# ConvNeXt-V2 block on one core: for 14 of 128 row blocks the residual x is copied to the output first and the result is added to it by accumulating transfers

## The chip, the cores and the metric

The kernel runs on one core of a Trainium2 chip. The core has five engines that work side by side, each with an instruction queue of its own that is worked off in order: TensorE (PE, with its weight loads listed as PEld), VectorE (DVE), ScalarE (ACT), GpSimd (POOL) and SyncE (SP). Here SP only issues transfers. GpSimd computes and issues transfers too. All transfers, whoever issues them, are carried by the core's 16 DMA engines.

The metric is the device time of one execution in microseconds (us). The kernel before has a median of 1466.34 us over three runs (1464.90 to 1467.73).

## The reference

x is an image of 512 x 512 pixels with C = 96 channels in bf16, w1 is 96 x 384, w2 is 384 x 96, and E = 384.

```python
out = sum over i, j of xp[:, i:i+H, j:j+W, :] * dw[i, j]     # 3x3 depthwise convolution
h = _layernorm(out, axis=-1)
h = gelu(h @ w1)                                             # tanh form, 384 channels
gx = sqrt((h * h).sum(over all pixels) + 1e-6)               # one number per channel
nx = gx / (gx.mean(over channels) + 1e-6)
h = grn_gamma * (h * nx) + grn_beta + h
return x + h @ w2
```

The sum over all pixels splits the work: no output can be formed before the hidden values of the whole image have been seen once. The scaling by gamma * nx + 1 is folded into w2 (the tile W2s), and beta @ w2 is one row of 96 numbers (B2c). So an output pixel is x + B2c + gelu(...) @ W2s.

## The kernel before, in words

The image is cut into 128 blocks of four rows (GR = 4, 2048 pixels, 384 KB of x). On the chip an output block lies as 128 partitions x 16 pixels x 96 channels.

**First phase.** A loop runs over slots s = 0 to last_slot. In slot s the 3x3 convolution of block s is made by matmuls, and the later steps of earlier blocks: statistics, the norm on GpSimd (tile yn), four writes of yn to a DRAM buffer, one read back in another layout (ynT), then the first product with w1 and the gelu (mlp). Each step has a slot from a small planner in the code: a write comes one slot behind its norm, the read one slot later, the mlp two slots behind the read. In this phase every engine's queue keeps the order of the program. The last mlp (block 127) is planned for slot 141, so slots 128 to 141 have no convolution any more. In those 14 slots SP issues what is left of the rows and broadcasts of the norm, the yn writes, the ynT reads and the stores of kept hidden values (`store_next`, g_dram); in slot 139 also the first five loads of x for the second phase (`load_xr`), in slot 141 the first calls of `load_rest`.

**Between the phases** VectorE works out the scaled W2s.

**Second phase.** A loop runs over n = 0 to 127, with q = ORDER[n] the block. ORDER mixes blocks whose hidden values are made again from ynT (three spread reads of 128 KB each, then matmuls and gelu into gr), blocks whose hidden values were stored (`gl`, one load of 1536 KB issued by GpSimd), and five that stayed in SBUF. From about the thirtieth block on every third one is a stored one in most stretches. For each n the program issues:

- `load_rest` and `load_xr` for n + 5: the hidden values, and x into the tile xr (384 KB, issued by GpSimd, five buffers);
- `stage_xb` for n + 2: GpSimd adds B2c to xr and writes xb in f32 (three buffers);
- `stage_mm2` for n: per block 48 matmuls of 96 columns in four parts, and for each part one VectorE addition of PSUM and xb into o_sb (bf16, four buffers); between the parts `pace` has PE and ACT make hidden values for later blocks;
- `stage_out` for n - 1: the store of o_sb, issued by SP.

PE, DVE and ACT keep the program's order. From n = 8 on the queues of SP and GpSimd in this phase are ordered by the scheduler of the language, by its own estimates and the dependencies.

In the profile nearly all instructions carry line 35, because a helper records them; the lines of the second phase that differ are L283 (xr load), L294 (gl load), L328 (xb), L128 (ynT reads) and L356 (store).

Of the kernel before, what the change touches and what calls it, by code (L numbers as in the profile page):

```python
# [8 lines left out]
ALU = mybir.AluOpType  # L9
# [3 lines left out]
GR = 4  # L13
# [43 lines left out]
def kernel(  # L57
# [10 lines left out]
    nc = tc.nc  # L68
# [5 lines left out]
    B, H, W, C = x.shape  # L74
# [6 lines left out]
    NBLK = H // GR  # L81
# [31 lines left out]
    PXP = GR * W // 128  # L113
# [11 lines left out]
    def read_spread(eng, t, q):  # L125
        rows = yn_dram[q].rearrange("(c i) (r w) -> i c r w", i=NI, r=GR)
        for i in range(NI):
            eng.dma_start(out=t[i:128:4], in_=rows[i])  # L128

    def yn_dst(q, r):  # L130
        return yn_dram[q].rearrange("(c i) (r w) -> r c i w", i=NI, r=GR)[r]
# [17 lines left out]
    B2bc_f = consts.tile([128, C], f32, name="B2bc_f")  # L149
# [9 lines left out]
    grp = {}  # L159
# [6 lines left out]
    B2c = consts.tile([128, C], f32, name="B2c")  # L166
# [3 lines left out]
    ORDER = []  # L170
# [16 lines left out]
    with ExitStack() as p1:  # L187
        pe, dve, act, pool, sp = (InOrder(tc, e) for e in (nc.tensor, nc.vector, nc.scalar, nc.gpsimd, nc.sync))
# [18 lines left out]
        def out_bank():  # L207
            out_banks[0] += 1
            return PS[:, 7 - out_banks[0] % 2, :GPS * C].rearrange("p (g c) -> p g c", g=GPS)
# [36 lines left out]
        for b in range(min(2, NBLK)):  # L246
# [3 lines left out]
                       in_=zrow[:, None, :NI * GR * 32].to_broadcast([128, 3, NI * GR * 32]), func=ACTF.Identity)  # L250
# [25 lines left out]
        GPS = max(d for d in range(1, cap + 1) if PXP % d == 0)  # L276
        NSUB = PXP // GPS

        def load_xr(n, pq):
            q = ORDER[n]  # L280
            r0 = q * GR
            xr = late.xr.tile([128, PXP, C], bf16, name="xr")
            pq.dma_start(out=xr[:], in_=x[0, r0:r0 + GR].rearrange("r w c -> (r w) c").rearrange(  # L283
                "(p g) c -> p g c", g=PXP))
            grp.setdefault(q, {})["xr"] = xr
# [35 lines left out]
                    c += sz  # L321
            act.activation(out=g[:, t, :, :].rearrange("p j w -> p (j w)"), in_=Uf, func=ACTF.Gelu_apprx_tanh)

        def stage_xb(q, pq, bias):
            if q is None:
                return
            xb = late.xb.tile([128, PXP, C], f32, name="xb")
            pq.tensor_tensor(out=xb[:], in0=grp[q]["xr"][:],  # L328
                                    in1=bias[:, None, :].to_broadcast([128, PXP, C]), op=ALU.add)
            grp[q]["xb"] = xb  # L330

        def stage_mm2(n, q):
            g, xb = grp[q]["g"], grp[q]["xb"]
            GQ = QW // 128
            o_sb = late.o.tile([128, PXP, C], bf16, name="o_sb")
            for sub in range(NSUB):
                O = out_bank()
                for gl_ in range(GPS):
                    gg = sub * GPS + gl_
                    for j in range(NCH):  # L340
                        t, c = gg // GQ, gg % GQ * 128
                        pe.matmul(O[:, gl_, :], lhsT=g[:, t, j, c:c + 128], rhs=W2s[:, j, :],
                                   start=(j == 0), stop=(j == NCH - 1))
                dve.tensor_tensor(out=o_sb[:, sub * GPS:(sub + 1) * GPS, :], in0=O,
                                   in1=xb[:, sub * GPS:(sub + 1) * GPS, :], op=ALU.add)
                if n == NBLK - 1:
                    out_part(q, o_sb, sub)
                if sub == NSUB - 1 and q in nth_made:
                    used[0] += 1
                pace(n, sub)  # L350
            grp.pop(q)
            return o_sb

        def stage_out(q, o_sb):
            r0 = q * GR
            nc.sync.dma_start(  # L356
                out=out[0, r0:r0 + GR].rearrange("r w c -> (r w) c").rearrange("(p g) c -> p g c", g=PXP),
                in_=o_sb[:])

        PRE = 5  # L360
        LEAD = 6
# [12 lines left out]
        def pace(n, sub):  # L374
            soon = (n, sub + 2) if sub < NSUB - 1 else (n + 1, 1)
            due = sum(1 for v in todo if v < soon or v[0] < n)
            even = LEAD + (n * NSUB + sub + 1) * total / (NSUB * NBLK)
            advance(max(due, even), n + PRE)
# [22 lines left out]
        for i in range(NI):  # L401
            dve.tensor_tensor(out=Wd[:, i], in0=eye32[:, None, :].to_broadcast([128, 9, 32]),
                              in1=Ud[:, i, :, None].to_broadcast([128, 9, 32]), op=ALU.mult)
        n = 0
        for h in range(2):
            for j in range(GR):
                for q in (2 * h, 2 * h + 1):
                    a = q + GR * shift(h, j) - j + 1
                    if 0 <= a < 3:
                        n += 1  # L410
                        o, i_ = Wq[32 * q:32 * q + 32, :, :, j, :], Wd[32 * q:32 * q + 32, :, 3 * a:3 * a + 3, :]
# [141 lines left out]
        def stage_newton(k, eng):  # L553
            N = BATCHES[k][1] * GR * NG
            var, rcur = rns[k]
            for it in range(NEWTON_ITERS):
                last = it == NEWTON_ITERS - 1
                t_ = small.tile([128, NS], f32, name="nt")
                eng.tensor_tensor(out=t_[:, :N], in0=rcur, in1=rcur, op=ALU.mult)
                eng.tensor_tensor(out=t_[:, :N], in0=t_[:, :N], in1=var[:, :N], op=ALU.mult)  # L560
                eng.tensor_scalar(out=t_[:, :N], in0=t_[:, :N], scalar1=-0.5, scalar2=1.5, op0=ALU.mult, op1=ALU.add)
                rn = small.tile([128, NS], bf16 if last else f32, name="rstd" if last else "rn")
                if last and N % 32:
                    eng.memset(rn[:, N:(N + 31) // 32 * 32], 0.0)
                eng.tensor_tensor(out=rn[:, :N], in0=t_[:, :N], in1=rcur, op=ALU.mult)
                rcur = rn[:, :N]
            rns[k] = rn
# [80 lines left out]
        def stage_write(b):  # L648
            yn = yns.pop(b)
            for r in range(GR):  # L650
                sp.dma_start(out=yn_dst(b, r), in_=yn[32 * r:32 * r + 32, :, :])
# [17 lines left out]
        def flat(b):  # L669
            return gs[b].rearrange("p t j w -> p (t j w)")  # L670
# [82 lines left out]
        def store_next():  # L753
            if stores:
                b, h = stores.pop(0)
                n = NCH * QW * NQ // 3
                sp.dma_start(out=g_dram[whole.index(b)][:, h * n:h * n + n],
                             in_=flat(b)[:, h * n:h * n + n])
# [9 lines left out]
        def gram_next(n):  # L768
            for b, c0 in grams[:n]:
                for c1 in (c0, c0 + E):  # L770
                    for j in range(NCH):
                        v = flat(b)[:, c1 + j * 128:c1 + j * 128 + 128]
                        pe.matmul(gram[:, j, :], lhsT=v, rhs=v, start=False, stop=True, skip_group_check=True)
            del grams[:n]
# [63 lines left out]
        for s in range(last_slot + 1):  # L838
# [9 lines left out]
            for b in get("write"):  # L848
                stage_write(b)
            store_next()  # L850
            for k in get("newton"):
                stage_newton(k, pool)
            for b in get("sqp"):
# [105 lines left out]
            if s == last_slot - 2:  # L959
                for n in range(PRE):  # L960
                    load_xr(n, sp)
            if s == last_slot - 1:
                for n in range(3):
                    stage_xb(ORDER[n], pool, B2bc_f)
            if s == last_slot:
                for n in range(PRE):
                    load_rest(n, sp, sp)
        while stores:
            store_next()
        gsm = p2.enter_context(tc.tile_pool(name="gsm", side="right", bufs=1))  # L970
        gram_next(len(grams))
        aggregate(NACC - 1)
# [14 lines left out]
        r = gi[:].bitcast(f32)  # L987
        for it in range(3):
# [5 lines left out]
            r = rn_[:]  # L994
# [21 lines left out]
    with p2:  # L1016
        def out_part(q, o_sb, sub):
            r0 = q * GR
            nc.sync.dma_start(
                out=out[0, r0:r0 + GR].rearrange("r w c -> (r w) c").rearrange(  # L1020
                    "(p g) c -> p g c", g=PXP)[:, sub * GPS:(sub + 1) * GPS],
                in_=o_sb[:, sub * GPS:(sub + 1) * GPS])

        held = None
        FIRST = 8
        for n, q in enumerate(ORDER):
            sq, pq = (sp, pool) if n < FIRST else (nc.sync, nc.gpsimd)
            if n + PRE < NBLK:
                load_rest(n + PRE, sq, pq)
                load_xr(n + PRE, pq)  # L1030
            if 3 <= n + 2 < NBLK:
                stage_xb(ORDER[n + 2], pq, B2c)
            if n == NBLK - 1:
                stage_out(*held)
                held = None
            o_sb = stage_mm2(n, q)
            if held:
                stage_out(*held)
            held = (q, o_sb)


# [28 lines left out]
```

## Time and profile before

| | |
|---|---|
| median of three runs | 1466.34 us |
| the profiled execution's own time | 1466.53 us |
| its span, first to last instruction | 1464.7 us |
| time outside the span | 1.83 us |
| mean granted TensorE clock | 0.998 |
| PE / ACT / POOL / DVE busy in the span | 95% / 96% / 89% / 80% |
| second phase | from about 965 us to the end |

The page gives the busy time of each engine, its course over 40 slices, the transfer queues, the chain of work that ended last, the costliest groups of instructions and the DMA issues. q0 is the queue of the transfers that GpSimd issues, q1 that of SP. Busy shares over the whole span mix two phases with different limits, so the second phase and the last 14 slots of the first are read in windows of their own. A DMA share is the mean busy share of the 16 DMA engines in a window.

### The profile page before, as it was taken

The numbers are of one execution on the slowest core, as the hardware profiler recorded it, in microseconds if no ns is written. First come the engines' busy times: TensorE is split into PE (matmuls) and PEld (weight loads), VectorE is DVE, ScalarE is ACT, GpSimd is POOL, SyncE is SP. The second block draws the span as 40 slices with busy tenths as digits, with TensorE's granted clock in tenths as the row PEclk, the third lists the DMA queues.
The fourth block names the chain that finished last, engine by engine and source line by source line (L and its number), as shares of the span: only waits on it lengthen the run. The fifth ranks groups of instructions, "written<-read, shape, count | busy, mean of one in ns | idle before, by whom it ended". The sixth has DMA issues, their size and how long they took to land.

```text
span 1464.7 us, 54551 instructions
## 1 busy us (share of the span) xinstructions
PE 1392.0 (95%) x23155; PEld 812.2 (55%) x23155; DVE 1176.8 (80%) x2163; ACT 1404.4 (96%) x1595; POOL 1300.3 (89%) x923
## 2 busy tenths in 40 slices
PE   8889999999999999999999998799999999999998
PEld 3434444444444444444444445567777777777766
DVE  7859989999999999999999998755555555555555
ACT  6889999999999999999999999999999999999997
POOL 2569889999999999999899998469999999999997
PEclk9999999999999999999999999999999999999999
DMA  5577878888888888888878777569999999999997
GB/s 173 166 232 246 252 247 254 259 263 269 256 268 284 248 260 265 273 259 265 257 249 272 247 240 217 171 215 386 348 332 393 393 398 390 402 384 406 388 380 306
DMA packets 167770, 421.66 MB, mean 288 GB/s; under 512 B 34278, under 2 KB 84134, under 8 KB 163046
## 3 DMA queue, kind: packets, MB, share of 16 engines
q1 hardware_dynamic: 151284, 314.59, 65.3%
q0 software_dynamic: 14880, 103.43, 18.6%
q8 instruction: 182, 2.98, 0.8%
q14 instruction: 62, 0.51, 0.1%
q10 hardware_dynamic: 1362, 0.15, 0.1%
HBM read 261.77 MB, written 156.22 MB: 285 GB/s over the span
## 4 chain that ended last, share of the span: by engine, by line
DVE 37%; PE 27%; ACT 13%; POOL 12%; DMA 5%; issue 4%; SPq 1%; ACTq 0%; POOLq 0%; DVEq 0%
PE PS L35 27%; DVE bst L35 26%; POOL xb L328 10%; ACT g L35 8%; DVE xT L35 7%; ACT y_bf L35 2%; DMA out_dram<-o_sb 2%; ACT xT L35 1%; ACT gr L35 1%; SPq L35 1%; POOL xr L283 1%; DMA yn_dram<-yn 1%; DVE y_bf L35 1%; DMA xin<-in_x_dram 1%; DVE o_sb L35 1%
## 5 line engine op out<-in xcount | busy, mean ns | idle before, releaser
L35 ACT ACTIVATE g<-PS 128x512 bf16<-128x512 f32 (+2 forms) x1054 | 718.8, 839 | 13.3 <-PE PS L35 10.1
L35 DVE BATCH_NORM_STATS2 bst<-g 128x6 f32<-128x512 bf16 x1098 | 665.8, 671 | 24.8 <-ACT g L35 24.6
L35 ACT ACTIVATE gr<-PS 128x1536 bf16<-128x1536 f32 x364 | 503.3, 1461 | 15.6 <-PE PS L35 11.0
L35 DVE TENSOR_TENSOR o_sb<-PS,xb 128x384 bf16<-128x384 f32 x512 | 277.7, 556 | 223.2 <-PE PS L35 177.3
L35 POOL TENSOR_TENSOR yn<-y_bf,rbc 128x1536 bf16<-128x1536 bf16 x126 | 391.4, 3109 | 47.2 <-ACT rbc L35 22.8
L328 POOL TENSOR_TENSOR xb<-xr,B2c 128x1536 f32<-128x1536 bf16 x118 | 368.2, 3134 | 1.5
L35 PE MATMUL PS<-xT,Wq 64*32 64x511 bf16 (+1 forms) x9198 | 345.2, 387 | 22.9 <-ACT y_bf L35 6.9
L35 PE MATMUL PS<-ynT,w1p 128*128 128x512 bf16 x1167 | 332.8, 381 | 22.4 <-ACT g L35 4.8
L35 POOL TENSOR_TENSOR ysq<-y_bf 128x1536 bf16<-128x1536 bf16 x114 | 313.4, 2749 | 30.7 <-ACT y_bf L35 17.4
L35 PE MATMUL PS<-ynT,w1s 128*128 128x512 bf16 x1008 | 272.3, 379 | 0.0
L35 PEld LDWEIGHTS <-gr 128*128 128x128 bf16 x4332 | 214.3, 98 | 62.6 <-issue 5.5
L35 PE MATMUL PS<-W2s,gr 128*128 128x96 bf16 x4224 | 223.4, 206 | 4.4 <-DVE o_sb L35 4.3
L35 PEld LDWEIGHTS <-Wq 64*32 64x32 bf16 x9216 | 111.7, 90 | 192.8 <-issue 151.1
L35 ACT ACTIVATE y_bf<-PS 128x1536 bf16<-128x1536 f32 (+2 forms) x135 | 182.2, 1355 | 16.1 <-PE PS L35 14.0
L35 DVE STREAM_TRANSPOSE xT<-xin 128x576 f32<-128x576 f32 (+1 forms) x256 | 181.3, 747 | 13.9 <-DMA xin<-in_x_dram 13.9
L35 PEld LDWEIGHTS <-w1p 128*128 128x128 bf16 x1167 | 89.9, 97 | 177.1 <-issue 105.8
L35 PEld LDWEIGHTS <-g 128*128 128x128 bf16 (+1 forms) x1659 | 102.4, 98 | 87.1 <-issue 56.1
L35 PE MATMUL PS<-w1p,ynT 128*128 128x384 bf16 (+2 forms) x834 | 127.2, 273 | 9.2 <-ACT xT L35 4.2
L35 PE MATMUL PS<-g 128*128 128x128 bf16 x1416 | 119.4, 221 | 3.6 <-DVE PS L35 3.6
L35 PEld LDWEIGHTS <-w1s 128*128 128x128 bf16 x1008 | 81.0, 98 | 40.0
L35 PEld LDWEIGHTS <-gl 128*128 128x128 bf16 x1680 | 83.0, 98 | 28.5 <-issue 7.1
L35 PE MATMUL PS<-W2s,gl 128*128 128x96 bf16 x1680 | 90.2, 206 | 3.9 <-DVE o_sb L35 3.4
(109 smaller groups left out, 723.2 us busy)
## 6 DMA issues: line engine op xcount, KB each, us to landing
xin<-in_x_dram SPq DMA_DIRECT2D x126, 432.0 KB
g_dram<-g SPq DMA_DIRECT2D x105, 512.0 KB
gl<-g_dram POOLq DMA_DIRECT2D x35, 1536.0 KB, 10.9
yn_dram<-yn SPq DMA_DIRECT2D x512, 96.0 KB
ynT<-yn_dram SPq DMA_DIRECT2D x128, 384.0 KB
out_dram<-o_sb SPq DMA_DIRECT2D x127, 384.0 KB
xr<-in_x_dram POOLq DMA_DIRECT2D x123, 384.0 KB, 6.6
ynT<-yn_dram SPq DMA_DIRECT2D x252, 128.0 KB
```

Source lines behind the costliest of these rows:

```text
L35: r = f(*a, **k)
L283: pq.dma_start(out=xr[:], in_=x[0, r0:r0 + GR].rearrange("r w c -> (r w) c").rearrange("(p g) c -> p g c", g=PXP))
L328: pq.tensor_tensor(out=xb[:], in0=grp[q]["xr"][:], in1=bias[:, None, :].to_broadcast([128, PXP, C]), op=ALU.add)
```

## The change

For the 14 blocks with n = 12, 20, 28 and so on to 116 in the order of the second phase (12 <= n < 120 and n % 8 == 4):

- in each slot from 128 on, behind `store_next`, SP issues one copy of x to out, DRAM to DRAM, for one of these blocks (384 KB). There are 14 such slots and 14 blocks, so the loop that would issue leftover copies behind the slots finds none;
- `load_xr` and `stage_xb` do nothing for them: no load of x into SBUF, no GpSimd addition;
- the four VectorE additions take B2c, broadcast over the pixels, in place of xb;
- the store of o_sb is issued by GpSimd, not SP, and adds o_sb to what lies in out.

The other stores have the same bytes as before and are written with flattened rows of 1536 numbers.

```diff
+    def px_rows(ap, r0):
+        return ap[0, r0:r0 + GR].rearrange("r w c -> (r w) c").rearrange("(p g) c -> p (g c)", g=PXP)
...
+        def adds(n):
+            return 12 <= n < 120 and n % 8 == 4
+
+        copied = [q for n, q in enumerate(ORDER) if adds(n)]
+
+        def copy_x():
+            if copied:
+                r0 = copied.pop(0) * GR
+                sp.dma_start(out=px_rows(out, r0), in_=px_rows(x, r0))
+
         def load_xr(n, pq):
             q = ORDER[n]
+            if adds(n):
+                return
...
-        def stage_xb(q, pq, bias):
-            if q is None:
+        def stage_xb(n, pq, bias):
+            q = ORDER[n]
+            if adds(n):
                 return
...
                 dve.tensor_tensor(out=o_sb[:, sub * GPS:(sub + 1) * GPS, :], in0=O,
-                                   in1=xb[:, sub * GPS:(sub + 1) * GPS, :], op=ALU.add)
+                                   in1=B2c[:, None, :].to_broadcast([128, GPS, C]) if adds(n)
+                                   else grp[q]["xb"][:, sub * GPS:(sub + 1) * GPS, :], op=ALU.add)
...
-        def stage_out(q, o_sb):
-            r0 = q * GR
-            nc.sync.dma_start(
-                out=out[0, r0:r0 + GR].rearrange("r w c -> (r w) c").rearrange("(p g) c -> p g c", g=PXP),
-                in_=o_sb[:])
+        def stage_out(n, o_sb):
+            o, v = px_rows(out, ORDER[n] * GR), o_sb[:].rearrange("p g c -> p (g c)")
+            if adds(n):
+                nc.gpsimd.dma_start(out=o, in_=v, accum_op=ALU.add)
+            else:
+                nc.sync.dma_start(out=o, in_=v)
...
             store_next()
+            if s >= NBLK:
+                copy_x()
...
         while stores:
             store_next()
+        while copied:
+            copy_x()
```

More of the change, by code (lines that the diff above doesn't have):

```diff
@@ L332, in stage_mm2 @@
         def stage_mm2(n, q):
-            g, xb = grp[q]["g"], grp[q]["xb"]
+            g = grp[q]["g"]
             GQ = QW // 128
@@ L963 @@
                 for n in range(3):
-                    stage_xb(ORDER[n], pool, B2bc_f)
+                    stage_xb(n, pool, B2bc_f)
             if s == last_slot:
@@ L1031 @@
             if 3 <= n + 2 < NBLK:
-                stage_xb(ORDER[n + 2], pq, B2c)
+                stage_xb(n + 2, pq, B2c)
             if n == NBLK - 1:
@@ L1038 @@
                 stage_out(*held)
-            held = (q, o_sb)
+            held = (n, o_sb)
 _INS = ['x', 'dw', 'w1', 'w2', 'grn_gamma', 'grn_beta']
```

## The prediction

> **What bounds the kernel now.** I first read the busy times by stage, because the shares over the span mix two phases. Columns: window, its length, busy us (and instructions) of PE, PEld, DVE, ACT, POOL, then the granted clock, the DMA share and GB/s.
>
> ```profile
> 877.00:943.00 66.00, 53.17 (x484) 33.87 (x483) 55.16 (x101) 65.02 (x49) 38.18 (x25) 0.97 0.67 201
> ...
> 1000.00:1128.00 128.00, 128.00 (x1880) 95.29 (x1877) 72.77 (x134) 126.61 (x93) 122.03 (x71) 1.00 0.97 364
> 1128.00:1250.00 122.00, 120.01 (x1749) 88.79 (x1746) 67.13 (x125) 118.15 (x86) 118.25 (x72) 1.00 1.01 395
> 1250.00:1379.00 129.00, 126.68 (x1844) 93.64 (x1843) 70.96 (x132) 124.73 (x91) 125.06 (x77) 1.00 1.01 393
> 1379.00:1420.00 41.00, 37.64 (x547) 27.60 (x546) 20.95 (x39) 37.16 (x28) 39.07 (x24) 1.00 1.02 395
> 1420.00:1455.00 35.00, 35.00 (x518) 26.10 (x516) 19.69 (x37) 34.69 (x27) 34.32 (x20) 1.00 0.96 368
> ```
>
> The first row is the stage that gets the copies: ACT is busy 65.0 of 66 us, POOL 38, the DMA engines 0.67. The others are the second phase. Up to 1128 and behind 1420 PE is never idle. Between, it loses 1.99 us (122 - 120.01), 2.32 and 3.36: together 7.67. That is all that a relief of other engines can give, since no PE work changes. Who takes it is in the waits from 1020 to 1440 us (waiter, releaser, total us, times, longest), and in the chain that ended last, cut at two places (start, us, what):
>
> ```profile
> DVE o_sb L35 <- PE PS L35: 144.2, 261, 0.7
> DVE o_sb L35 <- POOL xb L328: 36.4, 46, 1.5
> ...
> PE PS L35 <- DVE o_sb L35: 7.3, 16, 2.0
> DVE o_sb L35 <- DMA out_dram<-o_sb: 6.6, 3, 3.1
> ```
>
> ```profile
> 1141.05 6.21 POOL xb L328 x2
> 1147.77 0.54 POOL xr L283
> 1148.32 3.13 POOL xb L328
> ...
> 1379.50 13.40 DMA out_dram<-o_sb
> 1392.96 10.03 DMA out_dram<-o_sb
> ```
>
> From 1129 to 1379 the chain runs mostly through POOL: additions back to back with DMA issues, DVE waits for xb, PE for DVE. That is 4.31 us of PE. From 1379 to 1415 it runs through three stores that land 10 to 13 us after issue and hold o_sb: 3.36 us. So two limits lie close together, and the DMA engines are full (1.01) during both.
>
> **The change part by part.** The sum is made against the profiled execution: 1466.53 us, of which 1464.7 are span and 1.83 lie outside it; it is 0.19 us above the median of 1466.34. PE's granted clock stays at 1.00 in these stages and is left alone.
>
> ```profile
> L328 POOL TENSOR_TENSOR xb<-xr,B2c 128x1536 f32<-128x1536 bf16 x64 | 199.6, 3134 | 0.7
> L283 POOL DMA_DIRECT2D xr<-in_x_dram x64 | 35.4, 554 | 7.1 <-POOL xb L328 7.1
> L294 POOL DMA_DIRECT2D gl<-g_dram x20 | 10.7, 533 | 0.0
> ```
>
> POOL, per changed block (the rows are of 1128 to 1379 us): it loses one addition of 3.13 us, one xr issue of 0.55 and some 0.1 to 0.3 of gap, and gains one accumulating issue. No row shows such an issue. The nearest are xr and gl at 0.55 and 0.53, the same for 384 and for 1536 KB; I take 0.55, and twice that, 1.1, as the upper end, nothing as the lower. Net 2.6 to 4.0 us, about 3.2 in eight blocks. PE's loss to POOL is 4.31 us in 251 us, some 64 blocks, so 0.54 in eight blocks. POOL stops being the limit at either end.
>
> The accumulating issue waits on POOL for the fourth DVE addition of its block. Behind it stand xb of the third block after it, which waits for the same addition already (three buffers), and the xr and gl issues. xr lands in 6.7 us and is used about three blocks (11.7 us) after issue; gl lands in 11.1 with two buffers at one use per three blocks. A wait of a few us is covered; without that cover DVE would wait for it as it now waits for xb.
>
> DMA engines: at 393 GB/s with the engines full, 393,216 bytes take 1.00 us. A changed block loses the xr load and the plain store, 2.00 us. The accumulating transfer reads o_sb, reads out and writes out. Its price is not in the trace: one pass (1.00, the second read hidden) to three (3.00, each paid alone). I take two, since a copy already reads and writes in one pass and there are two reads. Balance 0, ends -14 to +14 us of DMA time over 14 blocks. The Trainium skill has a price here: "Collectives: The Full Stack", in the section on the bandwidth ceiling and the fold count, says that an add in the DMA path costs no cycles of its own but two source reads, and gives 62.28 against 32.35 GB/s, 1.93 to one; by it, as an estimate, the balance would be -1 us. No run here shows it yet.
>
> What full DMA engines allow: from 1128 to 1379 they carried about 394 GB/s at POOL's pace. The best 50 us of the phase had
>
> ```profile
> 1250.00:1300.00 50.00, 48.88 (x713) 36.06 (x712) 27.59 (x51) 48.03 (x36) 48.37 (x30) 1.00 1.01 399
> ```
>
> At 399 the 251 us shrink by 251 x (1 - 394/399) = 3.1 us, of at most 4.31. Lower end 0, if 394 is already the limit. I take 3.1.
>
> The stores: 14 of 128 leave SP's queue, which waits 55.9 us for earlier stores from 1050 to 1440 us. The bytes stay, so of the 3.36 us lost behind 1379 I take back a quarter, 0.8 (ends 0 and 3.36).
>
> o_sb: it has four buffers, so the accumulating transfer must land before DVE's first addition four blocks later: three blocks of 3.9 us and a quarter, 12.7 us after o_sb is full. It is issued 0 to 6.2 us late (two xb in a row), then lands as xr does (4.5, 6.7, 8.8: least, median, most) or behind a gl (up to 12.0), plus up to 2 us for the further passes. I take 1 + 8.7, which fits: cost 0. The far end is 20 us, 7 too late. A late store cost PE 3.36 us for 6.6 us of DVE waiting, 0.51 per us, so that end is 14 x 7 x 0.51 = 50 us.
>
> DVE: 56 additions read a broadcast B2c in place of xb, both f32. I take the row of xb, 556 ns, as the same; even at twice that DVE, 55% busy here, has room. The plain stores' flattened form moves the same bytes: 0.
>
> The copies: SP issues one in each of 14 slots, 0.3 to 0.6 us by the rows of its other issues, behind this slot's write and ahead of the next slot's rows, broadcasts and reads. On the DMA engines one is 1.0 us (read and write in one pass) to 2.0, 14 to 28 us, against 66 x 0.33 = 22 idle. What they push back is a ynT read: issued at 932.40 for block 126, whose gelu starts about 942.8, so 10 us of cover, less landing, for which I take xr's least 4.5; the first of these reads, issued at 878.64, has some 9 us to its gelu. POOL already waits 3.7 us at most for a broadcast there and is half idle. I take 0; ends 0 and +6 (28 - 22). No gain is possible there: ACT is the limit.
>
> Sum: -3.1 - 0.8 = -3.9 us, span 1460.8, time 1462.6.
>
> **The rivals.**
> - Full relief: the accumulating transfer costs one pass, the DMA engines get 14 us back and PE runs without a gap: -7.67, so 1458.9. For it: PE is at 100% at 1000 to 1128 us, with 364 GB/s. Against it: two reads.
> - No change: 394 GB/s is the limit, PE's waits move from xb to o_sb: 1466.5, plus or minus 2.5. For it: DMA share 1.01 for 290 us, and SP's queue waiting longer for stores as the phase goes on. The Trainium skill speaks for it: "DMA: Bandwidth & Descriptors", on issuing engines not being separate queues, says that giving a transfer to another engine saves only issue time, as all share 16 engines. By that rule moving the stores to GpSimd gives nothing; the trace agrees so far as q0 with 56.4% and q1 with 43.0% fill the engines together (1050 to 1440 us).
> - Slower, by the buffer: the accumulating transfers land late and hold o_sb. At 2 us beyond the 12.7, 14 x 2 x 0.51 = 14.3, less 3.9: 1476.9. It decides from about 1 us beyond on (7 us, the gain and the 2.9 of the bound). For it: the store's landing is at that edge already (13.4). Against it: GpSimd's xr lands in 6.7.
> - Slower, by the engines: three passes, +14 on full engines and no relief: 1480.
> - Slower, in the first phase: the copies cost two passes and the tail pays 6: 1468.6, up to 1472.5 if the gain is absent too.
>
> **How the numbers follow.** About 0.2%, 2.9 us, is what a measurement of this kernel can tell from no change. The forecast has 0.34 (own range 1460 to 1463.4), full relief 0.11, no change 0.20, the late buffer 0.20, three passes 0.10, the first phase 0.05. Faster 0.45, same 0.20, slower 0.35. The range goes from 1458 (full relief) to 1479: it leaves out the worse half of the late buffer and most of three passes, under 2 in 10.
>
> **What would show it.** POOL between 1100 and 1400 us below 92% busy, and DVE's 36 us of waiting for xb nearly gone; the DMA share still about 1.0 and near 399 GB/s; PE over 99%; the accumulating issues at 0.55 us, landing under 12 us; slots 128 to 141 as long as before and the second phase starting at 965. I am wrong if DVE waits for DMA on o_sb by tens of us, if the landing is beyond 13 us, if GB/s falls while the share stays at 1, or if the second phase starts later.

## The result, and the profile after

| | before | after |
|---|---|---|
| median of six runs | 1466.52 us (1464.90 to 1467.73) | 1510.07 us (1505.04 to 1518.57) |
| profiled execution / its span | 1466.53 / 1464.7 us | 1513.52 / 1511.6 us |
| mean granted TensorE clock | 0.998 | 0.98 |

The ratio is 1.030, with a 95% interval of 1.0267 to 1.0333: the kernel became 43.6 us slower. The forecast was 1462.6 us, in a range of 1458 to 1479.

The windows by stage of the kernel after, with the columns of the table in the prediction:

```profile
877.00:943.00 66.00, 51.14 (x486) 32.47 (x485) 55.74 (x100) 65.24 (x51) 41.18 (x25) 1.00 0.81 236
...
1000.00:1128.00 128.00, 115.72 (x1645) 85.58 (x1642) 63.74 (x118) 111.05 (x81) 101.51 (x62) 0.95 0.88 308
1128.00:1250.00 122.00, 105.69 (x1451) 77.62 (x1450) 56.14 (x104) 98.38 (x72) 89.58 (x58) 0.93 0.89 318
1250.00:1379.00 129.00, 127.03 (x1870) 94.56 (x1868) 71.85 (x133) 126.02 (x92) 115.56 (x73) 1.00 1.01 383
1379.00:1420.00 41.00, 39.01 (x546) 28.65 (x543) 20.86 (x40) 36.94 (x28) 34.03 (x21) 0.96 1.00 360
1420.00:1455.00 35.00, 33.36 (x491) 24.68 (x489) 19.00 (x35) 33.17 (x25) 30.37 (x20) 1.00 1.02 389
```

Before, PE lost nothing up to 1128 us and 7.67 us from 1128 to 1420. Now it is idle for 12.28 us in the second row shown, 16.31 in the third, 1.97 and 1.99 in the next two: 32.6 us together. And where the granted clock is below 1.00 its busy time buys less: 105.69 us for 1451 instructions are 72.8 ns each, where it was 68.6 (120.01 / 1749). Over the rows at 0.95, 0.93 and 0.96 this is 1645 x 2.3 ns + 1451 x 4.2 + 546 x 2.6 = 11 us. So some 44 us are lost here by this estimate, where 7.67 were lost before.

Who takes it is in the waits of the kernel after from 1000 to 1490 us (waiter, releaser, total us, times, longest):

```profile
POOL xb L344 <- DVE o_sb L35: 51.4, 31, 8.5
...
DVE o_sb L35 <- DMA out_dram<-o_sb: 44.1, 12, 8.8
PE PS L35 <- DVE o_sb L35: 34.1, 9, 7.7
```

The wait of 36.4 us for xb, which the change was to relieve, is no longer among the large ones. In its place DVE waits 44.1 us for transfers that still hold o_sb (6.6 before), PE waits 34.1 us for DVE (7.3 before), and GpSimd itself stands idle behind DVE. Which transfers these are is in the tile's own instructions, L374 being the new issue:

```profile
L374 POOL DMA_DIRECT2D out_dram<-o_sb x14: 907/923/946, 1024.1 to 1468.8; - x14
...
  DVE o_sb L35: 42.1, 8
DMA to landing us min/median/max: 7.8/10.7/13.8
```

The first line gives the least, median and greatest time in ns that GpSimd spends on one issue. The second, under "who waited for it", gives 42.1 of the 44.1 us to these 14 transfers, and to eight of them. A landing of 10.7 us at the median is longer than the 8.7 of the forecast, and the longest, 13.8, is inside the 14 that it allowed (12.0 behind a gl, and 2 for further passes). So the landing alone doesn't explain waits of 8 us. The course of DVE around the first such wait shows what does (start, us, what, and in brackets the idle time before it with its releaser):

```profile
1019.00 0.56 DVE L35 TENSOR_TENSOR o_sb<-PS,B2c 128x384 bf16<-128x384 f32 x1 [0.29 <-DMA out_dram<-o_sb]
...
1022.17 0.56 DVE L35 TENSOR_TENSOR o_sb<-PS,B2c 128x384 bf16<-128x384 f32 x1 [0.63 <-PE PS L35]
...
1038.02 1.02 DVE L35 TENSOR_TENSOR o_sb<-PS,xb 128x384 bf16<-128x384 f32 x2 [7.90 <-DMA out_dram<-o_sb]
...
1071.87 1.02 DVE L35 TENSOR_TENSOR o_sb<-PS,xb 128x384 bf16<-128x384 f32 x2 [6.55 <-DMA out_dram<-o_sb]
```

The first two lines are block n = 12: its o_sb is full at 1022.73. The accumulating transfer is issued at 1024.14 and lands 13.76 us later, at 1037.90; DVE goes on at 1038.02. Counting the additions in fours, the addition at 1038.02 is the first of block 15, not 16. The one at 1071.87 belongs to block 22 and waits for the buffer of block 20. The buffer was used again three and two blocks later, while three other buffers should have come first. For all 14 blocks, read from the semaphore that the first addition of each later block waits for:

| block n | landing, us | next use of its buffer | DVE waits, us |
|---|---|---|---|
| 12 | 13.76 | n + 3 | 7.90 |
| 20 | 9.36 | n + 2 | 6.55 |
| 28 | 7.80 | n + 3 | none |
| 36 | 11.46 | n + 2 | 8.81 |
| 44 | 13.45 | n + 3 | 7.46 |
| 52 | 9.98 | n + 3 | 3.38 |
| 60 to 116 (8 blocks) | 9.2 to 13.1 | n + 4 | 2.10, 2.75, 3.14; else about none |

Where DVE had nothing else to wait for, the addition that needs the buffer came 3.3 us after o_sb was full for n + 2, 7.3 to 7.4 for n + 3 and 11.3 for n + 4. The six transfers that GpSimd issues 0.5 us behind a gl load (n = 12, 44, 60, 76, 92 and 108) land in 11.8 to 13.8 us, the other eight in 7.8 to 11.5.

The chain of work of the kernel after runs through just these (start, us, what):

```profile
1024.14 13.76 DMA out_dram<-o_sb
...
1062.39 9.36 DMA out_dram<-o_sb
...
1131.42 11.46 DMA out_dram<-o_sb
...
1172.63 13.45 DMA out_dram<-o_sb
```

What such a wait does to PE, in short windows of the kernel after around the first one:

```profile
1024.00:1030.00 6.00, 6.00 (x87) 4.38 (x85) 3.57 (x7) 5.87 (x5) 4.64 (x4) 1.00 1.02 347
1031.00:1038.00 7.00, 0.84 (x8) 0.32 (x6) 0.00 (x0) 2.29 (x2) 2.89 (x2) 0.80 1.01 337
1038.00:1042.00 4.00, 3.37 (x30) 2.53 (x30) 1.58 (x3) 0.93 (x1) 0.00 (x0) 0.50 0.46 187
1042.00:1046.00 4.00, 4.00 (x59) 2.94 (x58) 2.23 (x4) 3.25 (x4) 3.12 (x1) 1.00 0.28 102
```

PE is idle for 6.16 of 7 us, and then does 30 instructions in 3.37 us where it later does 59 in 4.00: the granted clock is 0.50 for the first 4 us behind the wait. The Trainium skill, "TensorE: Matmul & The Clock Gate", Part 1 on the HAM clock gate, says that an idle stretch of about 3.4 us halves the clock until about 3.4 us of activity have gone by. The trace agrees: 0.50 behind 7.9 us of waiting, 1.00 again 4 us later. So a wait of 8 us costs about 2 us more than itself, and one of 2 us, as before had them, doesn't.

The end of the first phase moved too. Before, then after: SP's loads of x, GpSimd's first three additions, and two groups of DVE's additions that lead to W2s.

```profile
938.20 2.26 SPq L35 DMA_DIRECT2D xr<-in_x_dram  x5
...
942.47 9.28 POOL L35 TENSOR_TENSOR xb<-xr,B2bc_f 128x1536 f32<-128x1536 bf16 x3 [16.44 <-DMA xr<-in_x_dram]
...
951.86 0.27 DVE L35 TENSOR_TENSOR parts<-mom 128x78 f32<-128x78 f32 x1
...
952.16 0.57 DVE L35 TENSOR_TENSOR parts<-parts,mom 128x78 f32<-128x78 f32 x2
```

```profile
947.02 2.35 SPq L35 DMA_DIRECT2D xr<-in_x_dram  x5
...
953.96 9.33 POOL L35 TENSOR_TENSOR xb<-xr,B2bc_f 128x1536 f32<-128x1536 bf16 x3 [21.15 <-ACT gr L35]
...
954.63 2.57 DVE L35 TENSOR_TENSOR parts<-mom 128x78 f32<-128x78 f32 x1
...
957.24 6.18 DVE L35 TENSOR_TENSOR parts<-parts,mom 128x78 f32<-128x78 f32 x2
```

SP issues the loads 8.8 us later, with twelve copies ahead of them in its queue. GpSimd's additions end at 951.75 before and at 963.29 after, and now lie beside DVE's, which take 8.75 us in place of 0.84. The first o_sb of the second phase is written at 962.33 before and at 971.61 after. The run-up of the profiled execution was already 3.5 us longer before any of the copies (up to slot 128 the profiles here differ from the one before by -0.5 to +4.9 us). What is left to the copies is some 6 us.

### The profile page after: what moved, and what is told of

Same layout as the page of the kernel before. It is cut to its first block, busy times and chain, and to the rows that moved or that the text cites. A ratio compares the mean times of both kernels' runs of the same rounds, so it can differ in the third digit from the quotient of the medians.

```text
span 1511.6 us, 54539 instructions
## 1 busy us (share of the span) xinstructions
PE 1404.9 (93%) x23155; PEld 820.2 (54%) x23155; DVE 1185.2 (78%) x2163; ACT 1404.8 (93%) x1595; POOL 1263.2 (84%) x909
## 4 chain that ended last, share of the span: by engine, by line
DVE 32%; PE 31%; ACT 14%; POOL 9%; DMA 8%; issue 4%; SPq 1%; ACTq 0%; DVEq 0%; POOLq 0%
PE PS L35 31%; DVE bst L35 22%; ACT g L35 9%; DMA out_dram<-o_sb 7%; POOL xb L344 7%; DVE xT L35 6%; ACT y_bf L35 3%; POOL xr L298 1%; DVE o_sb L35 1%; DMA yn_dram<-yn 1%; DVE y_bf L35 1%; ACT gr L35 1%; ACT xT L35 1%; DVE parts L35 1%; POOL yn L35 1%
## 5 line engine op out<-in xcount | busy, mean ns | idle before, releaser
L35 DVE TENSOR_TENSOR o_sb<-PS,xb 128x384 bf16<-128x384 f32 x456 | 247.7, 557 | 234.5 <-PE PS L35 190.1
L344 POOL TENSOR_TENSOR xb<-xr,B2c 128x1536 f32<-128x1536 bf16 x104 | 325.4, 3132 | 54.9 <-DVE o_sb L35 52.8
L35 PE MATMUL PS<-xT,Wq 64*32 64x511 bf16 (+1 forms) x9198 | 348.8, 391 | 24.0 <-ACT y_bf L35 7.8
L35 PE MATMUL PS<-ynT,w1s 128*128 128x512 bf16 x1008 | 278.1, 386 | 0.0
L35 PEld LDWEIGHTS <-gr 128*128 128x128 bf16 x4332 | 217.6, 99 | 68.4 <-issue 13.3
L35 DVE STREAM_TRANSPOSE xT<-xin 128x576 f32<-128x576 f32 (+1 forms) x256 | 181.5, 749 | 11.5 <-DMA xin<-in_x_dram 11.5
```

The lines of the kernel that those rows point to most:

```text
L35: r = f(*a, **k)
L344: pq.tensor_tensor(out=xb[:], in0=grp[q]["xr"][:], in1=bias[:, None, :].to_broadcast([128, PXP, C]), op=ALU.add)
```

## The experiments

There were three questions. Is it the time for which a buffer is held, and of that the early second use or the longer landing? What did the relief of GpSimd bring by itself? And do the copies cost DMA time, or their place in SP's queue? Times move by some us with the run-up, so beside each time stands the row of the profile that it should show in. A profile shows one execution; the times are medians of 4 to 12.

### A buffer of its own for the 14 blocks

The kernel after, with one more buffer that only the adding blocks use (eight blocks apart). To make room, a scratch tile is laid over another.

```diff
+                late.oa = p2.enter_context(tc.tile_pool(name="oa", side="right", bufs=1))
...
-            o_sb = late.o.tile([128, PXP, C], bf16, name="o_sb")
+            o_sb = late.oa.tile([128, PXP, C], bf16, name="o_add") if adds(n) else late.o.tile(
+                [128, PXP, C], bf16, name="o_sb")
...
-            junk = bstpool.tile([128, 128], f32, name="junk")
+            junk = zrow[:].bitcast(f32)[:, :128]
```

> The change with one more tile for the result: the 14 adding blocks write into a buffer of their own (o_add), which is used again only eight blocks later (31 us); the other blocks keep their four. The scratch of the three diagonal products is moved onto a tile that is no longer used, to make room. Theory H (the accumulating transfer holds a buffer of o_sb that the second or third block behind it is given, and lands 9 to 14 us after issue): DVE's 44 us of waiting for out_dram<-o_sb fall below 8, the granted clock in the second phase is back at 0.99 or more, time 1462 to 1469. Theory T (the accumulating transfers overload the DMA engines wherever their result lies): the waits move to loads or to the plain stores, time stays above 1490. Theory C (the copies at the end of the first phase cost the time): above 1490 too.

Measured: 1465.79 us against 1466.32 for the kernel before in the same series, ratio 1.0004 (0.9979 to 1.0029). The 44 us are gone with this edit alone. Its wait and its windows:

```profile
DVE o_sb L35 <- DMA out_dram<-o_sb: 1.3, 2, 0.7
```

```profile
1128.00:1250.00 122.00, 122.00 (x1791) 90.79 (x1788) 69.53 (x128) 120.82 (x88) 111.15 (x71) 1.00 1.02 392
1250.00:1379.00 129.00, 128.97 (x1895) 96.07 (x1894) 73.08 (x135) 127.44 (x94) 117.53 (x74) 1.00 1.02 394
1379.00:1420.00 41.00, 41.00 (x611) 30.72 (x608) 23.28 (x43) 40.65 (x31) 37.21 (x25) 1.00 1.02 400
```

PE is idle for 0.03 us in all three and its clock is 1.00 throughout, though the accumulating transfers still land in 7.5 to 12.8 us. So the transfers, the issues on GpSimd and the missing additions together cost nothing in this execution, and the whole 7.67 us that PE lost before from 1128 to 1420 come back. Something else must take them again, since the median is no better than before. The copies are the first suspect. They can't be all of it: the profiled execution took 1462.00 us, and others of this kernel up to 1476.09 at a lower granted clock (0.989 where this one has 0.995). What those lose is in no profile.

### The same room for the kernel before

The kernel before with the scratch tile laid over in the same way, and five buffers in the pool (`bufs=4` becomes `bufs=5`).

> The kernel before with five buffers of o_sb in place of four and nothing else of the change (the same scratch moved). H: a fifth buffer only takes away the late stores behind 1379 us, 0 to 3.4 us, so 1463 to 1466.5; the difference of the own-buffer kernel to the change is then not worth of a buffer as such. If the number of buffers were worth tens of us in general, this kernel would be far under 1460.

Measured: 1466.77 against 1466.32, ratio 0.9998 (0.9986 to 1.0010). A fifth buffer doesn't help the kernel before (the forecast's upper end was 1466.5), and so the gain of the last experiment is not owed to the room alone.

### A plain store by GpSimd

The kernel after, with the 14 stores still issued by GpSimd but without adding, so that these blocks lack x.

```diff
-                nc.gpsimd.dma_start(out=o, in_=v, accum_op=ALU.add)
+                nc.gpsimd.dma_start(out=o, in_=v)
```

> The change with a plain store by GpSimd in place of the accumulating one (x is left out of the output of the 14 blocks, since the store overwrites the copy); copies, queue and buffers stay. H in the form that the early reuse of the buffer is what hurts: a plain store lands as xr does, 6.7 us or up to 12 behind a gl, the reuse after two blocks comes 8 us behind, so DVE still waits some 5 to 25 us for out_dram<-o_sb, time 1470 to 1495. H in the form that the second read makes it late: waits under 5 us, time 1463 to 1469. T: as the latter.

Measured: 1492.48 against 1466.32, ratio 1.0183 (1.0162 to 1.0204), with this wait:

```profile
DVE o_sb L35 <- DMA out_dram<-o_sb: 27.4, 9, 5.5
```

and the landing of the 14 stores:

```profile
DMA to landing us min/median/max: 6.3/9.9/12.0
```

DVE still waits 27.4 us for transfers that hold o_sb, 23.4 of them for these 14 and up to 5.5 at a time; that is a little over the 25 that were expected at most. Against the kernel with the buffer of its own this is 26.7 us of the 44.3: more than half of the loss doesn't need the addition in the transfer; the longer landing of the accumulating transfer adds 17.6 us (1510.07 - 1492.48). And the buffers are given out as before: the first additions of blocks 15, 22, 31, 38, 47 and 55 wait for the same six stores as in the kernel after. So the early second use does not come from the adding.

### Buffers strictly in turn

The kernel after with its four buffers as four pools, block n using number n mod 4. Only the order of use is changed; all engines work off their instructions and transfers in the same order as in the kernel after.

```diff
-                late.o = p2.enter_context(tc.tile_pool(name="o", side="right", bufs=4))
+                late.o = [p2.enter_context(tc.tile_pool(name=f"o{i}", side="right", bufs=1)) for i in range(4)]
...
-            o_sb = late.o.tile([128, PXP, C], bf16, name="o_sb")
+            o_sb = late.o[n % 4].tile([128, PXP, C], bf16, name="o_sb")
```

> The change with its four o_sb buffers used strictly in turn (block n takes buffer n % 4), so that the buffer of an accumulating block is due again four blocks later in every case, where the change gave it to the second or third block behind for n = 12 to 52. Copies, accumulating transfers and their landing stay. Theory H2 (the early hand-out makes most of the loss): the DVE waits on out_dram<-o_sb fall from 44 us to 5 to 20, time 1470 to 1480. Rival L (the late landing alone is enough): waits of 30 us or more, time 1490 or more.

Measured: 1474.74 against 1466.86, ratio 1.0058 (1.0037 to 1.0079).

```profile
DVE o_sb L35 <- DMA out_dram<-o_sb: 18.1, 9, 3.4
```

With the second use four blocks later every time, 35.3 us of the loss are gone (1510.07 - 1474.74). What stays is six waits of 2.2 to 3.5 us (16.5 of the 18.1), for the transfers of blocks 12, 44, 60, 76, 92 and 108. These land 13.4 to 14.7 us after o_sb is full, and the addition four blocks later needs the buffer 11.3 us after it, not 12.7 as the prediction had it; the other eight land within 11.2. The waits cost about the 9.0 us between this kernel and the one with the buffer of its own (1474.74 - 1465.79). So of the loss of 44.3 us the early second use makes 35 and the landing 9, if the early use is taken away first. Taken in the other order, by the plain store, the longer landing makes 17.6 and the early use 26.7: the two add to each other's waits.

### The relief alone

The kernel after without the copies, and with the 14 blocks stored by SP. They have neither load of x nor GpSimd's addition, and so they lack x.

```diff
             if adds(n):
-                nc.gpsimd.dma_start(out=o, in_=v, accum_op=ALU.add)
+                nc.sync.dma_start(out=o, in_=v)
...
-            if s >= NBLK:
-                copy_x()
...
-        while copied:
-            copy_x()
```

> The relief alone: the 14 blocks load no x, have no xb and no copy, and are stored by SP with a plain store (x is left out of the output of these blocks). If POOL's additions and nothing else bound the stretch from 1129 to 1379 us, PE runs there without a gap and the time is 1458 to 1460; if the DMA engines share the bound, the 5.5 MB less of loads help as well and nothing can be told from the time alone, but PE's idle time shows the limit of the gain: 7.7 us.

Measured: 1458.77 against 1466.86, ratio 0.9949 (0.9932 to 0.9967): 8.1 us, within the measurement the 7.67 that PE lost to other engines before.

```profile
1128.00:1250.00 122.00, 122.00 (x1794) 90.86 (x1791) 69.29 (x128) 120.86 (x88) 107.52 (x67) 1.00 1.01 394
1250.00:1379.00 129.00, 128.07 (x1873) 95.03 (x1872) 72.07 (x134) 126.85 (x93) 113.39 (x70) 1.00 1.00 387
1379.00:1420.00 41.00, 40.38 (x596) 29.93 (x594) 22.70 (x42) 39.84 (x30) 33.40 (x22) 1.00 1.01 389
```

PE is full in the first row, with the DMA share still 1.01 at 394 GB/s, and loses 0.93 and 0.62 us in the others. So a share of 1.01 did not mean that the DMA engines bounded the stage. All 128 blocks are stored by SP here, and none of them shows an early second use: the first additions of blocks 15, 22, 31, 38 and 47 wait for no store of two or three blocks before. With the plain stores above this ties the early use to GpSimd as the issuer.

### The copies alone

The kernel before with 14 copies of x of the same size, in the same slots of SP's queue, into a DRAM buffer that nobody reads (px_rows stands here for its body, written out).

```diff
             store_next()
+            if s >= NBLK:
+                sp.dma_start(out=side[s - NBLK], in_=px_rows(x, 8 * (s - NBLK)))
```

> The kernel before with 14 copies of x by SP in slots 128 to 141, into a side tensor in DRAM that nothing reads; nothing else of the change. H: the second phase starts some 2.4 us later, as in the change (967.4 against 964.9 us), time 1467 to 1470. C: 1485 or more.

Measured: 1473.06 against 1466.32, ratio 1.0049 (1.0028 to 1.0070). Its end of the first phase:

```profile
946.03 3.08 SPq L35 DMA_DIRECT2D xr<-in_x_dram  x5
...
951.76 9.34 POOL L35 TENSOR_TENSOR xb<-xr,B2bc_f 128x1536 f32<-128x1536 bf16 x3 [19.21 <-DMA xr<-in_x_dram]
...
955.04 6.19 DVE L35 TENSOR_TENSOR parts<-parts,mom 128x78 f32<-128x78 f32 x2
```

The time is above the range of 1467 to 1470 and far under the 1485 of theory C. The copies by themselves, with the 2.3 us that the run-up adds, move SP's loads by 7.8 us and GpSimd's additions by 9.3, and DVE's pair of additions takes 6.19 us as in the kernel after. Set against matching ACT instructions of the kernel before, the stretch from slot 128 to the first o_sb is 4.5 us longer here, 3.9 in the kernel with its own buffer, 5.8 in the kernel after, 4.1 with the plain store and 3.0 with the buffers in turn.

### The copies later

The same bytes, two of the copies in the last two slots and twelve behind them, so that all stand behind the loads of x in SP's queue; once in the kernel with its own buffer, once as side copies in the kernel before.

```diff
-            if s >= NBLK:
+            if s >= last_slot - 1:
                 copy_x()
```

> The own-buffer kernel with the copies issued later: none in slots 128 to 139, two in slots 140 and 141, twelve behind the slots, so that SP issues the five xr loads of slot 139 ahead of all of them. Theory Q (a copy's cost is its place in SP's queue: xr lands 8 us later, GpSimd's three xb then run beside VectorE's additions on parts, which take 2.6 to 3.1 us in place of 0.27): the additions are back under 0.4 us, the second phase starts within 1 us of before, time 1458 to 1461. Rival B (the cost is the 14 us of DMA time or of HBM traffic, wherever the copies stand): the second phase still starts 4 us or more late, time 1464 to 1469.

Measured: 1462.08 against 1466.86, ratio 0.9964 (0.9947 to 0.9980). This kernel beats both, the one before by 4.8 us. The time lies between the ranges of the two theories, so it decides for neither; the rows do.

```profile
942.97 2.26 SPq L35 DMA_DIRECT2D xr<-in_x_dram  x5
945.27 14.38 SPq L35 DMA_DIRECT2D out_dram<-in_x_dram  x14
...
947.26 9.28 POOL L35 TENSOR_TENSOR xb<-xr,B2bc_f 128x1536 f32<-128x1536 bf16 x3 [17.13 <-DMA xr<-in_x_dram]
...
955.58 1.09 DVE L35 TENSOR_TENSOR parts<-mom 128x78 f32<-128x78 f32 x1
956.70 0.58 DVE L35 TENSOR_TENSOR parts<-parts,mom 128x78 f32<-128x78 f32 x2
```

All 14 copies are now issued in one stretch at the boundary, and yet two additions are short again; the first takes 1.09 us, since GpSimd's three end at 956.54. From the first of the last twelve gelus to the first o_sb it takes 25.05 us; the kernel before takes 25.07. (In the second phase of this execution PE loses 2.75 us between 1128 and 1250, where DVE waits for stores.)

> The kernel before with the 14 copies into a side tensor that nothing reads, at the late places (slots 140 and 141 and behind the slots); nothing else of the change. Q: 1465 to 1468, against 1473.06 with the copies in slots 128 to 141. B: 1470 to 1475.

Measured: 1470.94 against 1466.86, ratio 1.0024 (1.0012 to 1.0035).

```profile
956.22 0.27 DVE L35 TENSOR_TENSOR parts<-mom 128x78 f32<-128x78 f32 x1
956.52 0.57 DVE L35 TENSOR_TENSOR parts<-parts,mom 128x78 f32<-128x78 f32 x2
```

The additions are as short as before and the same stretch takes 25.07 us, so the boundary bears out the place in the queue. The time does not: it should have been 1465 to 1468, and it lies in the range of the rival B (1470 to 1475). The profiled execution was 4.4 us late from its first 107 us on, and in the second phase, which took 2.2 us longer, DVE waits longer for GpSimd than the 36.4 us of the kernel before:

```profile
DVE o_sb L35 <- POOL xb L329: 60.5, 62, 2.2
...
POOL xr L284 <- POOL xb L329: 17.2, 58, 0.3
```

The scheduler put GpSimd's instructions of the second phase in another order there: in four places a load of x and an addition changed places. That this order cost the rest is argued from the waits, not tested. The copies alone kept the order of the kernel before and DVE waited 47.3 us for GpSimd there. So how much of the 4.1 us is still the copies' stays open.

## Why the prediction was wrong

**The step that failed** is that of o_sb: "it has four buffers, so the accumulating transfer must land before DVE's first addition four blocks later ... 12.7 us", at a cost of 0. The pool gave the buffer of the first six adding blocks to block n + 2 or n + 3, which left 3.3 or 7.3 us. With the buffers strictly in turn the second use comes four blocks later, as the step assumed, and the time is 35.3 us lower; even then the addition needs the buffer after 11.3 us and not 12.7, so the bound itself was 1.4 us too wide. What gives the buffer out so early is not the adding: plain stores by GpSimd lose the same six buffers, and with all stores on SP none is lost. Why the language does so for stores issued by GpSimd, and why the distance becomes four from block 60 on, stays open.

**The landing** was taken as 1 + 8.7 us from o_sb full. Measured: issued 0.3 to 1.6 us after, landing with a median of 10.7 and up to 13.8, the long ones behind a gl load. The forecast's 8.7 was a load's 6.7 and 2 for the adding; a plain store by GpSimd takes 9.9 at the median, so the load was the wrong row to start from, more than the adding. Even with the buffers in turn, six of 14 exceed the bound. The rival "slower, by the buffer" gave 1476.9 for 2 us beyond; buffers in turn measured 1474.74, with waits of 2.2 to 3.5 us. So this rival was right in the place and in the price of such waits: they cost 9.0 us for 18.1 us of waiting, 0.50 per us against the 0.51 taken. That its sum comes near is partly luck, since it took 14 late transfers where there were six, a gain of 3.9 where 8.1 was there, and nothing for the copies. It should have had more of the chances: the store that already took 13.4 us in the chain of the kernel before was the row to go by, not GpSimd's loads of x.

**The price per us of waiting**, 0.51, came from waits of at most 3.1 us, part of which PE had work to cover. Here 44.1 us of waiting cost about 44: PE waited 34.1 of them, so about 1 us of each of the 12 waits was covered, and the halved clock added 11. With the plain store, 27.4 us of waits of up to 5.5 us cost about 27 against the buffer of its own. A price from short waits doesn't carry to long ones.

**The relief of GpSimd** was right in kind and too small: 3.1 and 0.8 us for POOL and the stores, where 8.1 came with the relief alone and PE was full in the profile of the kernel with the buffer of its own. The step that was mis-sized is "what full DMA engines allow", which held that 399 GB/s was a limit. The kernel with its own buffer reaches full PE at 392 to 400 GB/s, and POOL is 91% busy from 1128 to 1379 (228.7 of 251 us), under the 92% named. The rival "no change" falls with it. The rule that goes with that rival, that the issuing engine saves only issue time, isn't touched, since the gain came from additions and loads left out, and not from who issues the store.

**Accumulating as two passes** was right. By the trace's single packets of 3072 bytes, an accumulating one takes 252 ns at the median and a plain store's 121: 2.08 to one. The Trainium skill's figure in "Collectives: The Full Stack", section on the bandwidth ceiling, was 1.93; the trace puts it a little higher. The issue on GpSimd took 0.92 us, between the 0.55 taken and the end of 1.1; POOL had room for it. The additions with B2c took 556 to 559 ns, as taken.

**The copies** were put at 0 because DMA time and the ynT reads had cover. At the boundary of the phases they cost 3 to 6 us, inside the ends of 0 to +6, but by a way that the step didn't look at: 0.6 us of SP's queue per copy, ahead of the loads of x of slot 139, which then start GpSimd's three additions late and beside DVE's. Of what stands behind a copy in that queue, only the ynT reads had been looked at. This holds for the boundary: its stretch is 3.0 to 5.8 us longer in the five profiles with early copies, and no longer than before in the two with late ones. The medians follow only in part. Late copies still cost the kernel before 4.1 us (6.7 when early), and the kernel with its own buffer and late copies is 3.3 us above the relief alone; what makes these is not shown. The rival "slower, in the first phase" had the size (6), by luck, with another mechanism.

**The sum**, in place of -3.9 us, as an estimate from the rows above: about +6 by the copies, -7.7 by the relief, +44 by the held buffers with the clock: 1466.5 + 42 = 1509, measured 1510.07.

## What to carry to other kernels

Before a store is replaced by a longer transfer, find out which later tile gets its buffer by the waits of the instructions and not by the count of buffers; if another engine issues it than its neighbours, give it a buffer of its own. Price a wait by its length: one that outlasts the work queued on TensorE costs all of itself, and some of the clock behind it. A transfer put into a queue costs first what stands behind it there, and whether the DMA engines have room is the second question.

## What was not expected of the hardware

DVE's additions on `parts` (128x78, both inputs in SBUF) took 0.27 us alone, and 2.6 to 3.1 us each while GpSimd was adding x and B2bc_f into xb, three of them in the kernel after: as long as one of GpSimd's additions (3.1 us). One of them alone is covered: the relief alone had one of 3.23 us, and its stretch to the first o_sb took 25.07 us as before. The Trainium skill, "SBUF — State Buffer", section on who interferes with whom, says that a VectorE instruction with two SBUF inputs contends with a GpSimd instruction that reads SBUF, and that the loser is blocked for the other's whole instruction. The trace agrees. The additions into o_sb, with one input from PSUM, stayed at 0.56 us beside the same GpSimd work.
